# Loading the last sum of w2 into a separate buffer one unit sooner, and turning the last two quarter blocks together at the end: routing attention with a feed-forward block on one Trainium2 core

## The chip, the cores and the metric

The kernel runs on one core of a Trainium2 chip. A core has five engines, each with its own queue of instructions: TensorE (PE, with its weight loads shown as PEld), VectorE (DVE), ScalarE (ACT), GpSimd (POOL) and SyncE (SP). SP, ACT and POOL also issue transfers (DMA) between the device memory and the core's own memories: SBUF, from which the engines work, and PSUM, eight banks into which TensorE writes its sums. The metric is the time on the device in microseconds (us) of one execution.

## What is computed

```python
# attention: batch 4, 8 heads, 768 rows, 64 columns; a key counts where its nearest of 16
# centroids is the query's
mask = q_assign[:, :, :, None] == k_assign[:, :, None, :]
scores = np.where(mask, scale * q @ k.transpose(0, 1, 3, 2), -1e9)
attn = softmax(scores)
x = (attn @ v) as (4, 768, 512)
# feed-forward block, w_ch1 512x2048, w_ch2 2048x512
xn = (x - mean) / sqrt(var + 1e-6) * g_ln
out = x + np.maximum(xn @ w_ch1, 0.0) @ w_ch2
```

All of it is in 32-bit floats.

## The kernel before

**Stages.** First the attention of 16 pairs of heads (to 318 us of the span), then the feed-forward block for each batch b of 0 to 3, 768 rows each. Both products of the feed-forward block use fewer multiplications than the plain method: they are split into 2x2 blocks and done as seven block products (Winograd's form of Strassen's scheme), whose operands are sums and differences of blocks. For b of 1 to 3 the second product is split twice: seven products of seven products, 49 in all.

**The first product of a batch** runs in eight units j of 0 to 7 (`first_units`, L1355; `first_layer`, L897). In a unit TensorE makes seven products of 1.29 us each (L855, into the banks `x_ps`, `y_ps`, `z_ps`), ScalarE copies some of them out (L881) and applies the rectifier (L894, L922), and VectorE adds others (L886) and then makes sums of the hidden blocks (`outer_sums`, L1099 to L1102). Between the units stands `unit_end` (L1463), which for b = 1 does more: it prepares w2 for the second layers.

**Preparing w2 (b = 1).** Four sums of blocks of w2 were written to device memory earlier (`w2_keep`, into `w2_t`). Each comes back by `w2_back(i)` (L1040; one transfer of 1 MB issued by SP, L1042) into a buffer of the pool `splits` with tag "t", of which there is one. `w2_split(m, src)` (L1056) then makes four differences of it on VectorE (L1063, into the tile `wt`, two buffers) and stores them with one transfer of 1 MB issued by SP (L1064, into `w2_d`). The order over the units j = 0 to 6 is m = 1, 5, 3, 4, 2, 7, 6; m = 5, 4, 7, 6 read a sum that came back, m = 1, 3, 2 read w2 itself. Sum 1 is asked for ahead of the units, sums 4, 3 and 2 at the end of units 1, 3 and 5, after the split in that unit. In the profile's names digits are left out, so `w_t` stands both for the buffer and for the memory it is loaded from, `w_d` for `w2_d`.

**The second product** (`deep_layer`, L1227) goes through 49 steps (m, way); each is a `deep_product` (L1134) of 1.30 us on TensorE (L1146). Its weights come through a ring of ten slots filled by `ring_load` (L1080, one transfer of 256 KB, L1088, issued by SP). The first ten loads are asked for at the end of units 5, 6 and 7, the others one per step. After each step VectorE or ScalarE takes the bank out (L1159 copy, L1161 add), and `inner_sums` (L1120, L1122) and `inner_late` (L1127, L1129) make operands for later steps. Step (4, 1) stands ahead of the last work of the first layer, which follows as a job of steps (4, 1) and (4, 2).

**The buffers with tag "sums"** (pool `xpool`, two buffers of 128 x 2304 floats). In the first units of b = 1 one of them holds the sums `xt` of the input blocks. The other was last the tile `w2t`, read by TensorE (L963) in the second layer of b = 0. The next tile taken with this tag is `qs` in `inner_sums`, in unit 7.

**The end of the program** (b = 3). The outputs of the last m = 3 are sent out quarter by quarter by `last_part` (L1242). For ways 2 and 7 VectorE transposes a block of 32 x 32 pieces and four transfers send it (L1266, L1270). For ways 4 and 3, the last two steps, the quarter block lies in `end` (128 x 192, L1161); TensorE transposes its two halves through an identity (L1255) into the PSUM tile `turned`, VectorE copies the first half to `y_end` and ScalarE the second (L1259), and SP sends the first half and ACT the second (L1260, 48 KB each). `turned` comes from a PSUM pool of two banks (`ps_n`, L838), `y_end` from six buffers (`unit`).

**Order.** In this part of the program the instructions of PE, DVE, ACT and SP run in the order in which the code writes them; the waits between engines are put in by the framework, per tile. So a wait at the head of one queue holds up all that is written behind it on the same engine.

At the very end every engine loads the flag that tells whether a rarely used general path is needed (L1535) and branches over that path (L1536); then SP waits for the transfers and the other engines (L1759).

Of the kernel before, what the change touches and what calls it, by code (L numbers as in the profile page):

```python
# [23 lines left out]
def kernel(  # L24
# [49 lines left out]
    def ps(name, dt=F32, n=512):  # L74
        p = pools["long" if "long" in pools and name in ("x_ps", "z_ps") else "t"]
        return p.tile([P, n], dt, tag="t", name=name)
# [961 lines left out]
        nc.sync.dma_start(out=w2_t[i - 1], in_=t.rearrange("p h c f -> p (h c f)"))  # L1038

    def w2_back(i):  # L1040
        t = splits.tile([P, 2, NFH, P], F32, tag="t", name="w2_t")
        nc.sync.dma_start(out=t.rearrange("p h c f -> p (h c f)"), in_=w2_t[i - 1])  # L1042
        return t

    def w2_whole():

# [180 lines left out]
    def deep_layer(b, more, st):  # L1227

        done = {}

        def ahead_of(m):
            p = st[m] = {}
            onto = {2: 1, 3: 5}.get(m)
            p["add"] = done.get(onto)
            p["to"] = done[m] = done[onto] if onto else unit(f"m{m}")
            if m == ORDER[-1] and not more:
                p["ends"] = {}

        def sum_onto(i, j):
            nc.vector.tensor_tensor(done[i], done[i], done[j], ALU.add)  # L1240

        def last_part(o, way):  # L1242

            part = {2: (0, 0), 7: (1, 1), 4: (1, 0), 3: (0, 1)}.get(way)
            if part is None:
                return
            r, j = part
            queues = (nc.sync, nc.scalar, nc.gpsimd, nc.gpsimd) if way == 7 else (nc.sync, nc.scalar)
            if way in (4, 3):

                columns = st[ORDER[-1]]["ends"][way]
                turned, y = ps("turned"), unit("y_end")
                n = QC // 2
                for i in range(2):
                    nc.tensor.transpose(  # L1255
                        turned[:n, i * P : (i + 1) * P], columns[:, i * n : (i + 1) * n], ident
                    )
                    copy = (nc.vector.tensor_copy, nc.scalar.copy)[i]
                    copy(y[:n, i, :P], turned[:n, i * P : (i + 1) * P])  # L1259
                    (nc.sync, nc.scalar)[i].dma_start(  # L1260
                        out=out[b, r * QC + i * n : r * QC + (i + 1) * n, MH + j * P : MH + (j + 1) * P],
                        in_=y[:n, i, :P],
                    )
                return
            y = unit("y_end")[:, 0, :QC]
            nc.vector.transpose(y, o[:, j].rearrange("p (t a r) -> p t a r", a=2, r=Q)[:, :, r])  # L1266
            to = out[b].rearrange("(a r t) m -> a (r t) m", r=Q, t=NT)[r]
            for i in range(P // Q):
                m = MH + j * P + i * Q
                queues[i % len(queues)].dma_start(  # L1270
                    out=to[:, m : m + Q], in_=y[i * Q : (i + 1) * Q].rearrange("r (t f) -> r t f", f=Q)
                )

        def between():
            first_layer(b, NFH - 1, 3)
            relu(len(summed))
            outer_sums(NFH - 1, True)
            if more:
                norm_load(b + 1, 0)

        def s4(n):
            return lambda: outer_late((1, 1), (0, 1), "s", n)

        def norm(i, c):
            return lambda: norm_apply(b + 1, i, c)

        def rest(r, k, m):
            return lambda: add_rest(b, r, k, done[m])

        def out_of(r, k, m):  # L1290
            return lambda: turn(b, r, k, done[m])

        def onto(i, j):
            return lambda: sum_onto(i, j)

        jobs = {
            (4, 1): [lambda: first_layer(b, NFH - 1, 4)],
            (4, 2): [between],
            (4, 5): [lambda: rest_load(b, 0)],
            (4, 3): [rest(1, 0, 4)],  # L1300
            (7, 6): [s4(0)], (7, 4): [s4(1)], (7, 3): [s4(2)], (1, 6): [s4(3)],
            (1, 4): [onto(4, 7)], (6, 3): [onto(6, 1)],
            (5, 4): [onto(4, 6)], (5, 3): [onto(5, 6)], (2, 6): [onto(7, 5)],
        }
        for i, m in enumerate(ORDER[1:]):
            for n, way in enumerate((5, 7)):
                jobs.setdefault((ORDER[i], way), []).append(lambda m=m, n=n: inner_sums(st, m, (n,)))
        if more:
            for at, (i, c) in (
                ((4, 4), (0, 0)), ((7, 5), (0, 1)), ((1, 3), (0, 2)), ((6, 6), (0, 3)),  # L1310
                ((6, 5), (1, 0)), ((6, 4), (1, 1)), ((5, 6), (1, 2)), ((5, 5), (1, 3)),
            ):
                jobs.setdefault(at, []).append(norm(i, c))
            for at, c in (((4, 7), 1), ((7, 2), 2), ((7, 3), 3)):
                jobs.setdefault(at, []).append(lambda c=c: norm_load(b + 1, c))
            jobs[2, 4] = [out_of(1, 0, 4)]
            jobs[2, 3] = [rest(0, 0, 2), lambda: rest_load(b, 1)]
            jobs[3, 6] = [lambda: x_sum(b + 1, 1)]
            jobs[3, 5] = [lambda: w1_sums(b + 1, 0, (0, 1))]
            jobs[3, 7] = [lambda: first_layer(b + 1, 0, 1)]  # L1320
            jobs[3, 4] = [lambda: x_sum(b + 1, 2)]
            later(
                rest(1, 1, 7), out_of(1, 1, 7), out_of(0, 0, 2), None,
                rest(0, 1, 3), out_of(0, 1, 3), None,
            )
        else:
            jobs[7, 2] = [lambda: rest_load(b, 1)]
            jobs[1, 3] = [rest(1, 1, 7)]
            jobs[5, 6] = [rest(0, 0, 1), onto(4, 6)]
            del jobs[5, 4]  # L1330
            jobs[2, 5].append(rest(0, 1, 5))
            jobs[2, 1] = [out_of(1, 0, 4)]
            jobs[2, 7].append(out_of(1, 1, 7))
            jobs[2, 3] = [out_of(0, 0, 2)]

        for m, way in STEPS:
            if way == 1:
                ahead_of(m)
            deep_product(st, m, way)
            ring_load(b)  # L1340
            leave(2 if more else 4, (nc.sync,) if more else (nc.sync, nc.scalar))
            if way == 1:
                inner_late(st, m, way)
            for job in jobs.get((m, way), ()):
                job()
            if way == 2:
                inner_late(st, m, way)
            if m == 3 and not more:
                last_part(done[m], way)
        leave(len(leaving))  # L1350
        places[1, 1], places["e"] = places["e"], places[1, 1]

# [105 lines left out]
    with tc.manual_schedule(engines=order | {mybir.EngineType.SP}):  # L1458
# [4 lines left out]
        def unit_end(b, j):  # L1463

            if b + 1 < B:
                if j == 0:
                    rows_load(b + 1, 1)
                if j < NT:
                    norm_rows(b + 1, j)
            if b == 1:  # L1470
                leave(4)
                if j == 0:
                    outer["ends"] = all_in_range()
                if j == 2:
                    outer["flag"] = flag_of(outer.pop("ends"))
                m = (1, 5, 3, 4, 2, 7, 6, None)[j]
                if m in SUMS:
                    w2_split(m, outer.pop("t"))
                elif m:
                    w2_split(m, by_half(w2_block(*{1: (0, 0), 2: (1, 0), 3: (1, 1)}[m])))  # L1480
                if j in (1, 3, 5):
                    outer["t"] = w2_back({1: 4, 3: 3, 5: 2}[j])
                if j in (5, 6):
                    outer_late("s", "e", (0, 0), j - 5)
            while pending:
                job = pending.pop(0)
                if job is None:
                    break
                job()
            if b + 1 < B and j + 3 == NFH:  # L1490
                norm_stats(b + 1)
            if b + 1 < B and j + 2 == NFH:
                norm_stat_rows(b + 1)
            leave(4)
            if b == 1:
                if turning and j % 2 == 0:
                    columns_turn(row, lambda out, in_: leaving.append((out, in_)))
                elif asked and j % 2:
                    columns_load(row)
            if j > 4:  # L1500
                for _ in range(4):
                    if ring["next"] < len(STEPS) * (b - 1) + RING:
                        ring_load(b)

        for b in range(1, B):
# [1 line left out]
            if b + 1 < B:  # L1507
                rows_load(b + 1, 0)
            if b == 1:
                outer["t"] = w2_back(1)  # L1510
                first_units(b, 0)
            else:
                first_layer(b, 0, 2)
# [250 lines left out]
```

## Time and profile before

| what | us |
|---|---|
| median of 3 runs | 885.56 (885.01 to 886.95) |
| the profiled execution | 885.48 |
| its span, first to last instruction | 883.7 |
| PE busy in 534.20 to 552.00 (17.80 us) | 16.66 |
| DVE busy in 534.20 to 552.00 | 13.92 |
| PE busy in 552.00 to 600.00 (48.00 us) | 48.00 |
| PE busy in 600.00 to 740.00 (140.00 us) | 140.00 |
| PE busy in 740.00 to 872.00 (132.00 us) | 131.77 |
| PE busy in 872.00 to 884.00 (12.00 us) | 4.13 |

The span is the time from the first to the last instruction of one profiled execution; some 1.8 us of the execution's own time lie outside it. The table gives TensorE's busy time by stretches: where it is near the length of the stretch, TensorE had work all the time, and the difference is what it stood still. The granted clock was 1.00 in each of these stretches but the last.

### The profile page before, as it was taken

To read this page: it belongs to the slowest core of one execution; us is meant where nothing else is said; L and a number is where in the kernel's file an instruction comes from. 1 tells how busy PE (TensorE), PEld (TensorE's weight loads), DVE (VectorE), ACT (ScalarE), POOL (GpSimd) and SP (SyncE) were. 2 spreads that over 40 slices of the span, in tenths; PEclk is the share of its full clock that TensorE was granted. 3 is DMA by queue.
4 is the path that set the end of the run, shared out by engine and by line. 5 is a ranking of instruction groups with operands and counts; after the bars stand their busy time and mean duration, and the time that the engine had idled before them with its cause. 6 is when DMAs were issued, how large, how long until landed. Compare 5 with 4: busy or idle time off the path is not lost.

```text
span 883.7 us, 13207 instructions
## 1 busy us (share of the span) xinstructions
PE 871.6 (99%) x4648; PEld 574.7 (65%) x4648; DVE 704.5 (80%) x1149; ACT 402.8 (46%) x741; POOL 78.3 (9%) x143
## 2 busy tenths in 40 slices
PE   8999999999999999999999999999999999999996
PEld 5444444444444445568885557996557997557995
DVE  6899999999999878959577778997556897646774
ACT  6777788888898823330004542103552101333110
POOL 1012121222222212110000000000000000000000
PEclk9999999999999999999999999999999999999998
DMA  7777899999986338875685878854236862511874
GB/s 161 135 130 127 152 173 184 196 208 183 196 190 186 99 116 210 232 202 208 187 193 163 251 246 304 294 160 98 57 72 207 282 191 54 119 54 39 276 200 99
DMA packets 250426, 151.01 MB, mean 171 GB/s; under 512 B 192096, under 2 KB 207984, under 8 KB 249328
## 3 DMA queue, kind: packets, MB, share of 16 engines
q1 hardware_dynamic: 219216, 130.75, 56.1%
q0 software_dynamic: 7776, 15.03, 8.8%
q10 hardware_dynamic: 23360, 4.30, 2.7%
q8 instruction: 39, 0.64, 0.3%
q14 instruction: 35, 0.29, 0.1%
HBM read 108.40 MB, written 33.25 MB: 160 GB/s over the span
## 4 chain that ended last, share of the span: by engine, by line
PE 97%; DVE 1%; DMA 1%; ACT 0%; issue 0%; ACTq 0%
PE x_ps L855 18%; PE s_ps L401 18%; PE a_ps L413 14%; PE x_ps L1146 12%; PE z_ps L855 9%; PE z_ps L1146 6%; PE x_ps L963 5%; PE y_ps L855 5%; PE y_ps L1146 3%; PE z_ps L963 2%; PE sim_ps L320 1%; PE den_ps L469 1%; PE y_ps L963 1%; DMA k_sb<-in_k_dram 0%; DMA q_sb<-in_q_dram 0%; ACT lower L894 0%
## 5 line engine op out<-in xcount | busy, mean ns | idle before, releaser
L401 PE MATMUL s_ps<-t,t 64*128 64x384 f32 x768 | 154.8, 483 | 0.0
L401 PEld LDWEIGHTS s_ps<-t,t 64*128 64x128 f32 x768 | 68.0, 187 | 39.0 <-issue 38.3
L1146 PE MATMUL x_ps<-lower,w 128*128 128x192 f32 x448 | 80.9, 327 | 0.5 <-DVE u L1161 0.4
L1146 PEld LDWEIGHTS x_ps<-lower,w 128*128 128x128 f32 x448 | 74.1, 190 | 2.5 <-DVE u L1161 0.7
L886 DVE TENSOR_TENSOR lower<-z_ps,u 128x384 f32<-128x384 f32 x56 | 31.0, 553 | 53.1 <-PE z_ps L855 42.9
L396 ACT ACTIVATE e<-s_ps 128x768 f32<-128x768 f32 x84 | 67.0, 811 | 7.0 <-PE s_ps L401 6.4
L396 ACT ACTIVATE w<-s_ps 128x768 f32<-128x768 f32 x80 | 64.4, 811 | 8.3 <-PE s_ps L401 7.7
L894 ACT ACTIVATE lower<-lower 128x384 f32<-128x384 f32 x88 | 44.8, 521 | 45.9 <-DVE lower L886 45.8
L401 PE MATMUL s_ps<-mask,mask 64*128 64x384 bf16 x384 | 62.7, 323 | 1.0 <-ACT e L396 0.6
L881 ACT COPY u<-x_ps 128x384 f32<-128x384 f32 x64 | 30.5, 477 | 67.2 <-PE x_ps L855 67.1
L413 PE MATMUL a_ps<-e,v_sb 128*64 128x384 f32 x336 | 57.6, 488 | 0.0
L413 PE MATMUL a_ps<-w,v_sb 128*64 128x384 f32 x320 | 55.2, 488 | 0.0
L881 ACT COPY p<-x_ps 128x384 f32<-128x384 f32 x32 | 15.0, 470 | 83.6 <-PE x_ps L855 82.1
L855 PE MATMUL x_ps<-xn,ws 128*128 128x384 f32 x128 | 46.6, 487 | 0.0
L855 PE MATMUL x_ps<-xn,w 128*128 128x384 f32 x128 | 46.6, 487 | 0.0
L855 PE MATMUL x_ps<-xt,ws 128*128 128x384 f32 x128 | 46.6, 486 | 0.0
L855 PE MATMUL y_ps<-xn,w 128*128 128x384 f32 x128 | 46.5, 486 | 0.0
L855 PE MATMUL z_ps<-xt,ws 128*128 128x384 f32 x128 | 46.5, 486 | 0.0
L855 PE MATMUL x_ps<-xt,w 128*128 128x384 f32 x128 | 46.5, 486 | 0.0
L855 PE MATMUL z_ps<-xn,ws 128*128 128x384 f32 x128 | 46.5, 486 | 0.0
L1270 POOL DMA_DIRECT2D out_dram<-y_end x2 | 1.2, 597 | 487.5 <-DMA out_dram<-y 487.5
L413 PEld LDWEIGHTS a_ps<-e,v_sb 128*64 128x64 f32 x336 | 23.5, 137 | 31.8 <-issue 29.9
(232 smaller groups left out, 1679.4 us busy)
## 6 DMA issues: line engine op xcount, KB each, us to landing
w<-w_d SPq DMA_DIRECT2D x84, 256.0 KB, 3.2
raw<-in_moe_w_ch_dram SPq DMA_DIRECT2D x32, 512.0 KB, 4.7
w<-w_t SPq DMA_DIRECT2D x36, 256.0 KB, 5.1
w<-tb POOLq DMA_DIRECT2D x32, 256.0 KB, 5.4
w_d<-wt SPq DMA_DIRECT2D x7, 1024.0 KB, 5.6
w<-w_all SPq DMA_DIRECT2D x27, 256.0 KB, 2.8
v_sb<-in_v_dram SPq DMA_DIRECT2D x32, 192.0 KB, 5.2
xr<-x_d SPq DMA_DIRECT2D x24, 256.0 KB, 2.9
```

What stands on the lines that cost most here:

```text
L320: nc.tensor.matmul(sim[r : r + Q, :HC], cT[:, pr, :, :].rearrange("p j c -> p (j c)"), prepared[n][side][:, g * HC : (g + 1) * HC], start= ...
L396: nc.scalar.activation(e, s[:, :, :HC], AF.Exp, scale=SCALE)
L401: nc.tensor.matmul(s[:, j, :HC], of_keys[:, keys], of_queries[:, o : o + HC], start=part == first, stop=part != first, skip_group_check=True,)
L413: nc.tensor.matmul(acc[j * D : (j + 1) * D, :HC], loaded[n]["v"][:, j, c, :], e[:, j, :], start=(c == 0), stop=(c == NT - 1),)
L469: nc.tensor.matmul(den[r : r + Q, :HC], ones, sums[n, g][h][:, j, :], start=h == 0, stop=h == parts - 1, tile_position=(0, r), skip_group_ ...
L855: nc.tensor.matmul(bank[:, :HC], lhs[:, c, :], rhs[:, c], start=first and c == 0, stop=c == NDH - 1, skip_group_check=True,)
L881: nc.scalar.copy(t, bank[:, :HC])
L886: nc.vector.tensor_tensor(h, bank[:, :HC], other, ALU.add)
L894: nc.scalar.activation(h, h, AF.Relu)
L963: nc.tensor.matmul(bank[:, :MH].rearrange("p (h f) -> p h f", h=2), hidden[lhs + (c,)][:, tt * P : (tt + 1) * P], rhs[:, :, c], start=firs ...
L1146: nc.tensor.matmul(bank, w[:, c, :], a[:, c], start=way in (1, 2, 5) and c == 0, stop=c == NQH - 1, skip_group_check=True,)
L1270: queues[i % len(queues)].dma_start(out=to[:, m : m + Q], in_=y[i * Q : (i + 1) * Q].rearrange("r (t f) -> r t f", f=Q))
```

## The change

Three edits.

1. `w2_back` no longer returns its buffer but notes it under the sum's number, so that two may be under way. Sum 2, the last to come back, goes into a buffer with tag "sums" instead of the one with tag "t", and is asked for at the end of unit 4 instead of unit 5.
2. At the end, nothing is done after step (3, 4). After step (3, 3) `last_part` is called for way 4 and then for way 3.
3. In `last_part` each half gets its own PSUM tile `turned`, and the engines are dealt anew: both halves of way 4 are copied by ScalarE and sent by SP; of way 3 the first half is copied by VectorE and sent by SP, the second copied by ScalarE and sent by ACT, as before.

```diff
     def w2_back(i):
-        t = splits.tile([P, 2, NFH, P], F32, tag="t", name="w2_t")
+        if i == 2:
+            t = xpool.tile([P, 3, S], F32, tag="sums", name="w2_t", bufs=2).rearrange("p a s -> p (a s)")
+            t = t[:, : NFH * MH].rearrange("p (h c f) -> p h c f", h=2, c=NFH)
+        else:
+            t = splits.tile([P, 2, NFH, P], F32, tag="t", name="w2_t")
         nc.sync.dma_start(out=t.rearrange("p h c f -> p (h c f)"), in_=w2_t[i - 1])
-        return t
+        outer["t", i] = t
...
-                turned, y = ps("turned"), unit("y_end")
-                n = QC // 2
+                n, y = QC // 2, unit("y_end")
                 for i in range(2):
-                    nc.tensor.transpose(
-                        turned[:n, i * P : (i + 1) * P], columns[:, i * n : (i + 1) * n], ident
-                    )
-                    copy = (nc.vector.tensor_copy, nc.scalar.copy)[i]
-                    copy(y[:n, i, :P], turned[:n, i * P : (i + 1) * P])
-                    (nc.sync, nc.scalar)[i].dma_start(
+                    turned = ps("turned")
+                    nc.tensor.transpose(turned[:n, :P], columns[:, i * n : (i + 1) * n], ident)
+                    copy = nc.vector.tensor_copy if way == 3 and i == 0 else nc.scalar.copy
+                    copy(y[:n, i, :P], turned[:n, :P])
+                    (nc.sync if way == 4 or i == 0 else nc.scalar).dma_start(
...
             if m == 3 and not more:
-                last_part(done[m], way)
+                for part in {4: (), 3: (4, 3)}.get(way, (way,)):
+                    last_part(done[m], part)
...
                 if m in SUMS:
-                    w2_split(m, outer.pop("t"))
+                    w2_split(m, outer.pop(("t", SUMS.index(m) + 1)))
...
-                if j in (1, 3, 5):
-                    outer["t"] = w2_back({1: 4, 3: 3, 5: 2}[j])
+                if j in (1, 3, 4):
+                    w2_back({1: 4, 3: 3, 4: 2}[j])
...
             if b == 1:
-                outer["t"] = w2_back(1)
+                w2_back(1)
                 first_units(b, 0)
```

## Prediction

> **What bounds it now.** The page first: TensorE's busy time, and the chain that ended last.
>
> ```profile
> PE 871.6 (99%) x4648; PEld 574.7 (65%) x4648; DVE 704.5 (80%) x1149; ACT 402.8 (46%) x741; POOL 78.3 (9%) x143
> PE 97%; DVE 1%; DMA 1%; ACT 0%; issue 0%; ACTq 0%
> ```
>
> TensorE is the bound; only what it waits for, and what follows it at the end, can be won. Next, its waits, longest first (those over 0.6 us):
>
> ```profile
> PE turned L1255 <- DVE end L1161: 1.2, 2, 0.6
> PE y_ps L1146 <- ACT lower L894: 1.1, 1, 1.1
> PE idle_ps L700 <- DVE warm L176: 1.0, 1, 1.0
> PE turned L1255 <- DVE y_end L1259: 0.8, 2, 0.4
> ```
>
> The second must be traced back, through three timelines (start, duration, idle before and who ended it). TensorE's:
>
> ```profile
> 536.81 1.14 PE L1146 MATMUL y_ps<-lower,w 128*128 128x192 f32 x6
> 539.08 0.59 PE L1146 MATMUL y_ps<-lower,w 128*128 128x192 f32 x2 [1.13 <-ACT lower L894]
> 540.97 1.54 PE L1146 MATMUL x_ps<-lower,w 128*128 128x192 f32 x8
> 542.35 1.46 PE L1146 MATMUL z_ps<-qs,w 128*128 128x192 f32 x8
> ```
>
> VectorE's, which makes the hidden blocks for that step:
>
> ```profile
> 526.73 0.55 DVE L886 TENSOR_TENSOR lower<-z_ps,u 128x384 f32<-128x384 f32 x1
> 529.91 0.69 DVE L1063 TENSOR_TENSOR wt<-w_t 128x512 f32<-128x512 f32 x1 [2.62 <-DMA w_t<-w_t]
> ...
> 534.92 0.56 DVE L1099 TENSOR_TENSOR fifth<-lower 128x384 f32<-128x384 f32 x1 [0.59 <-ACT lower L894]
> ...
> 537.92 0.55 DVE L886 TENSOR_TENSOR lower<-z_ps,u 128x384 f32<-128x384 f32 x1
> ```
>
> And SP's, which asked for what VectorE waits for:
>
> ```profile
> 510.85 0.37 SPq L1064 DMA_DIRECT2D w_d<-wt  x1
> 515.01 2.13 SPq L1219 DMA_DIRECT2D x_d<-col  x4
> 521.91 0.38 SPq L1064 DMA_DIRECT2D w_d<-wt  x1
> 522.33 0.50 SPq L1042 DMA_DIRECT2D w_t<-w_t  x1
> ```
>
> Read from below: SP asks for sum 2 at 522.33, behind the 1 MB store of 521.91; it lands at 529.82 (landings are from the trace's records of completed transfers). VectorE, free since 527.29, stands 2.62 us. Everything behind its split comes late, to the add at 537.92; the rectifier of that block ends at 539.02, and TensorE, at the last chunk of step (4, 2), has waited. Last, the end on TensorE and ACT:
>
> ```profile
> 872.22 1.57 PE L1146 MATMUL x_ps<-lower,w 128*128 128x192 f32 x8 [0.45 <-DVE u L1161]
> 874.38 0.31 PE L1255 MATMUL turned<-ident,end 128*96 128x128 f32 x1 [0.59 <-DVE end L1161]
> 875.08 0.31 PE L1255 MATMUL turned<-ident,end 128*96 128x128 f32 x1 [0.38 <-DVE y_end L1259]
> 875.23 1.47 PE L1146 MATMUL z_ps<-lower,w 128*128 128x192 f32 x8
> 878.62 0.33 ACTq L1260 DMA_DIRECT2D out_dram<-y_end  x1
> ```
>
> Product (3, 3) stands behind two turns that wait for VectorE.
>
> **Part A, sum 2 earlier.** The same 1 MB load, none added. In SP's queue it is moved past the w_d store of 521.91 and the four x_d stores of 515.01, to directly behind the store of 510.85: issue at 511.3. ACT's and POOL's queues aren't passed. SP stands idle there until 515.01, so nothing in its queue waits longer, if the buffer is free. It is: its last tenant `w2t` was last read by TensorE (L963) at 454, and the other "sums" buffer, `xt`, read until 537, isn't touched. The next tenant, `qs` (written at 536.46), then waits for VectorE's own split only. Landing: 7.5 us after issue as now, 518.8; even the slowest landing of these transfers in the stretch, 8.8, gives 520.1, before 527.29. What the load displaces: the x_d stores land some 2.7 us later (sum 2 landed that much behind the store ahead of it, 527.13 to 529.82), and nobody reads them in this batch. The transfer that VectorE awaits at 514.01 (`col`, issued at 504.83, landed 513.88) is ahead of it in the queue and keeps its place.
>
> Now VectorE afresh from 527.29, with its own durations: split 2.54 us to 529.85, `outer_late` to 530.72, the y add to 531.18; then it waits for TensorE's z product (ends 531.80), adds to 532.37, waits for the rectifier to 532.95, `outer_sums` and `inner_sums` to 535.95, the last z add to 536.5. Rectified at 537.05, where TensorE asks at 537.79: the wait goes, with 0.7 us to spare (if that cover fails, each us of it costs one). Then `inner_sums` for the last chunk (537.09 to 537.82) and `inner_late` to 538.85; step (4, 6) would ask at 539.40. So that small wait goes too. What TensorE gains: from 536.81 to 542.35 it took 5.54; without waits it is 1.30 + 1.29 + 1.30 = 3.89 (products' starts lie 1.30 and 1.29 apart elsewhere). **1.65 us.** The low end is the wait as listed, 1.13; that nothing is won, or something lost, are rivals below. The nearest row to the value is the sum of the products itself, so I take the high end.
>
> What is late next? In the stage from 534 to 552 the transfers are busy 91%. I paired each ring load with its product: the load for (4, 7) lands at 542.84, 0.81 us before its use at 543.65; all others in this batch have 1.4 and more. TensorE comes there 1.65 earlier, at 542.0. But that load is issued at 537.95, behind a load that waits for the tiny statistics store queued behind the split's 1 MB store (532.56). That store moves 2.6 us earlier with VectorE, and with it these issues: landing near 540.2, 1.8 us to spare. From 552 on TensorE stands nowhere until 871.8, so the gain reaches the end.
>
> **Part B, the end.** Four turns, four copies and four stores remain; one copy goes from VectorE to ACT, one store from ACT to SP. Product (3, 3) follows (3, 4) directly: start 873.63 (872.22 + 1.41), last matmul done 875.09. `end` of way 4 was ready at 874.33, in its cover. The turns of way 4 run at 874.93 and 875.08 (0.15 is what follows a turn at 875.08); ACT's two copies (0.26 each) end at 875.56 and 875.82, and hold up nothing else on ACT, which stood idle 16 us; SP sends. `end` of way 3: 875.13 to 875.63 (0.50). Its first turn 875.68 to 876.0, VectorE's copy (0.29) to 876.32, SP's issue 876.38. Its second turn adds a wait, for the bank of way 4's second half, free at 875.82 (nothing stands behind it on TensorE): 875.87 to 876.18, ACT's copy to 876.48, ACT's issue 876.51 instead of 878.62. So ACT and TensorE end 2.11 earlier. SP's last issue was at 877.95, and is now third in a row (0.33 to 0.35 each, from 875.59), held by the copy: 876.38, **1.57 earlier**.
>
> After that 4.7 us pass in which no view shows work. The trace's records of branches and semaphores, which no view prints, show: each engine branches (VectorE 878.27, SP 878.33, TensorE 878.56, ACT 879.53), resumes 2.7 to 3.8 us later, and SP checks all transfers until 882.83. The last store's landing at 881.9 (3.3 after issue, most of it in 1.5) held SP 0.44 us. New: SP branches at 876.77, resumes at 879.46, needs 1.37 of unheld checks: 880.83, 2.0 earlier. The store lands by 879.8, in cover (879.95 is when SP would ask). POOL's drain, though, ended at 881.06 and depends on none of this: against 882.93 it allows 1.87. I take **1.9**, range 1.2 to 2.2. The far bounds: SP's issues at the 1.03 us that one took amid small-packet stores at 868.88 would put its last end 0.4 later than now; the nearest row, 0.34 for this very form, speaks for the other end.
>
> The Trainium skill, "DMA: Bandwidth & Descriptors", section "Issuing engines are not separate DMA queues", holds that all issuing queues share the same 16 DMA engines and several of them only save issue time: by it, a third store on SP costs one issue and nothing else, which the trace's 0.34 us puts inside the copy's wait. "Runtime: NRT & Kernel Launch", section "Instruction fetch mechanics", says that a taken branch to a page not held forces a fetch before going on; the 2.7 to 3.8 us after the branches agree, and by it the end would move with the latest branch, ACT's, by 2.1 rather than by 1.9.
>
> **Sum.** 1.65 + 1.9 = 3.55. The profiled execution took 885.48 (span 883.7 and 1.8 around it): 881.9; on the median of 885.56, **882.0**.
>
> **Rivals.**
> - *A is given back* (8%): the load or another late operand takes the wait's place. For: 0.81 us of slack now. Against: its issue moves more than its use. Time 885.56 - 1.9 = 883.7.
> - *The end doesn't move* (7%): fetches after the branches, or the landing among four stores within 1 us, set it. For: landings up to 4.4 us in this trace, a DMA share of 0.94 at 874 to 875. Against: 0.46 by 876. Time 885.56 - 1.65 = 883.9.
> - *The buffer isn't free and SP asks no sooner, nor does the end move* (3%): 885.6. The tenants' last reads speak against it.
> - *Slower* (4%): the ring runs dry at (4, 7). TensorE waits there for each us that the load lands after 542.0; to eat 3.55 and 1.8 more it must land after 547.3, against 542.84 now. Two bursts of 1 MB ahead of it (2.7 each, some 5.4) bring it to 548.2, 6.2 too late: 885.56 - 3.55 + 6.2 = 888.2. For: 91% busy transfers. Against: the 1 MB that stood just there is moved away.
>
> **The numbers.** 78% for the forecast, whose own range (A 1.13 to 1.65, B 1.2 to 2.2, 0.5 for the spread of medians) is 881.2 to 883.7. With the two lesser gains 8 in 10 lie in 880.9 to 884.0. About 0.2%, 1.8 us, can be told from no change, so faster means under 883.8: the forecast and more than half of the first rival, some of the second: 85%; same 11%; slower 4%.
>
> **What would show it.** VectorE's split of sum 2 starts near 527.3 with no wait for `w_t`; L1146's wait for L894 is gone; step (4, 6) starts near 539.4; product (3, 3) follows (3, 4) at 1.4; the last ACT issue comes 2.1 earlier relative to (3, 4). Wrong would be a wait of TensorE on a ring load near 542, or a gap of more than 4.9 us after the last issue.

## The result, and the profile after

| | before | changed |
|---|---|---|
| median of 11 runs each, us | 886.06 (885.01 to 887.16) | 883.25 (882.74 to 884.20) |
| the profiled execution, us | 885.48 | 882.89 |
| its span | 883.7 | 881.1 |
| start of the span to step (4, 1) | 534.22 | 534.56 |
| step (4, 1) to step (3, 4) | 338.00 | 336.29 |
| step (3, 4) to the end | 11.49 | 10.26 |

The ratio of the times is 0.9971, with a 95% interval of 0.9962 to 0.9980: 1.8 to 3.4 us less. Forecast was 882.0 in a range of 880.9 to 884.0, from a median before of 885.56 that came out 0.5 higher here. The last three rows are starts of TensorE's steps in the two traces. The first of them ends ahead of the first wait of TensorE that the change removes; in the kernels below it lies anywhere between some 534 and 535.6, with the new load or without, and this noise has to be taken out before two profiles are compared. What is left is a gain of 1.71 us in the middle (forecast 1.65) and of 1.23 us at the end (forecast 1.9).

**The page** (busy time with its share of the span and its instructions, then the chain that ended last):

```profile
PE 871.2 (99%) x4648; PEld 575.4 (65%) x4648; DVE 703.9 (80%) x1148; ACT 403.3 (46%) x742; POOL 77.9 (9%) x143
...
PE 99%; DVE 0%; ACT 0%; issue 0%; ACTq 0%
```

TensorE does the same work in 871.2 us, of a shorter span. One copy has gone from DVE to ACT (1149 to 1148 instructions, 741 to 742). TensorE's longest waits of 500 us and later are now these (line, whom it waits for; total, times, longest):

```profile
PE turned L1259 <- ACT y_end L1261: 0.5, 1, 0.5
PE x_ps L1150 <- DVE u L1165: 0.4, 1, 0.4
```

(Four lines were added ahead of them, so L1146, L1161 and L1255 are now L1150, L1165 and L1259.) The wait of 1.1 us for the rectifier L894 is gone, and so are the four waits of the turns for VectorE, 2.0 us in all. One wait of a turn for a bank has come, as the prediction said it would.

**The middle.** SP's timeline (start, duration), then VectorE's, then TensorE's:

```profile
511.18 0.37 SPq L1068 DMA_DIRECT2D w_d<-wt  x1
511.65 0.45 SPq L1046 DMA_DIRECT2D w_t<-w_t  x1
515.46 4.56 SPq L1223 DMA_DIRECT2D x_d<-col  x4
522.35 0.38 SPq L1068 DMA_DIRECT2D w_d<-wt  x1
...
530.75 1.90 SPq L608 DMA_DIRECT2D stat_d<-st  x1
535.54 0.80 SPq L611 DMA_DIRECT2D stat_row<-stat_d  x2
536.39 0.42 SPq L1092 DMA_DIRECT2D w<-w_d  x1
```

```profile
527.17 0.55 DVE L886 TENSOR_TENSOR lower<-z_ps,u 128x384 f32<-128x384 f32 x1
527.64 0.68 DVE L1067 TENSOR_TENSOR wt<-w_t 128x512 f32<-128x512 f32 x1
```

```profile
537.15 1.46 PE L1150 MATMUL y_ps<-lower,w 128*128 128x192 f32 x8
538.45 1.45 PE L855 MATMUL z_ps<-xn,ws 128*128 128x384 f32 x4
539.74 1.46 PE L1150 MATMUL x_ps<-lower,w 128*128 128x192 f32 x8
541.04 1.46 PE L1150 MATMUL z_ps<-qs,w 128*128 128x192 f32 x8
```

SP asks for sum 2 at 511.65, directly behind the store of unit 4. VectorE's split starts at 527.64, right after the add, with no bracket behind it: it waited for nothing. On TensorE the chunk y_ps, which was torn in two with 1.13 us between, is one group of eight, and the starts lie 1.29 to 1.30 apart.

**The end** (TensorE, VectorE, and the issues of SP and ACT):

```profile
870.85 1.57 PE L1150 MATMUL x_ps<-lower,w 128*128 128x192 f32 x8 [0.45 <-DVE u L1165]
...
872.26 1.46 PE L1150 MATMUL z_ps<-lower,w 128*128 128x192 f32 x8
...
873.56 0.38 PE L1259 MATMUL turned<-ident,end 128*96 128x128 f32 x2
873.76 0.50 DVE L1165 TENSOR_TENSOR end<-z_ps,u 128x192 f32<-128x192 f32 x1 [0.80 <-PE z_ps L1150]
...
874.15 1.49 SPq L1262 DMA_DIRECT2D out_dram<-y_end  x3
...
874.40 0.40 PE L1259 MATMUL turned<-ident,end 128*96 128x128 f32 x2 [0.46 <-ACT y_end L1261]
...
875.13 0.35 ACTq L1262 DMA_DIRECT2D out_dram<-y_end  x1
```

Product (3, 3) starts 1.41 us after (3, 4), and the last issue of ACT lies at 4.27 us after the start of (3, 4), where it was 6.40: 2.13 earlier, forecast 2.11. All of this went as predicted. But from the end of that issue, 875.48, to the end of the span, 881.1, there are 5.6 us, where there were 4.8: a good part of what was won ahead of the last issue is lost behind it.

### The profile page after: what moved, and what is told of

It is laid out like the page before. It is cut to its first block, busy times and chain, and to the rows that moved or that the text cites. A ratio compares the mean times of both kernels' runs of the same rounds, so it can differ in the third digit from the quotient of the medians.

```text
span 881.1 us, 13202 instructions
## 1 busy us (share of the span) xinstructions
PE 871.2 (99%) x4648; PEld 575.4 (65%) x4648; DVE 703.9 (80%) x1148; ACT 403.3 (46%) x742; POOL 77.9 (9%) x143
## 4 chain that ended last, share of the span: by engine, by line
PE 99%; DVE 0%; ACT 0%; issue 0%; ACTq 0%
PE x_ps L855 19%; PE s_ps L401 18%; PE a_ps L413 14%; PE x_ps L1150 12%; PE z_ps L855 9%; PE z_ps L1150 6%; PE x_ps L963 5%; PE y_ps L855 5%; PE y_ps L1150 3%; PE z_ps L963 2%; PE sim_ps L320 1%; PE den_ps L469 1%; PE y_ps L963 1%; PE idle_ps L700 0%; PE qk_ps L303 0%
## 5 line engine op out<-in xcount | busy, mean ns | idle before, releaser
L1150 PE MATMUL x_ps<-lower,w 128*128 128x192 f32 x448 | 80.8, 326 | 0.4 <-DVE u L1165 0.4
L1150 PEld LDWEIGHTS x_ps<-lower,w 128*128 128x128 f32 x448 | 74.2, 190 | 2.1 <-DVE u L1165 0.7
L894 ACT ACTIVATE lower<-lower 128x384 f32<-128x384 f32 x88 | 44.9, 521 | 43.7 <-DVE lower L886 43.7
```

Source lines behind the costliest of these rows:

```text
L894: nc.scalar.activation(h, h, AF.Relu)
L1150: nc.tensor.matmul(bank, w[:, c, :], a[:, c], start=way in (1, 2, 5) and c == 0, stop=c == NQH - 1, skip_group_check=True,)
```

## The experiments

The question is what becomes of the 2.1 us at the end, and which edit each gain belongs to. All times at the end are counted from the start of step (3, 4), so that kernels can be laid side by side; those of branches, landings and POOL's drain are from the trace's records of branches, semaphores and completed transfers, which no view prints. "Resumes" is SP's first instruction behind its branch, and POOL's drain is the long instruction in which POOL waits after its last work. In e10 and e11 that drain lay far ahead of the end: it was over at 496.3 and 393.4 us of the span.

| kernel | last issue | SP branches | SP resumes | last landing | POOL's drain ends | end |
|---|---|---|---|---|---|---|
| before | 6.40 | 6.11 | 8.80 | 9.72 | 8.83 | 11.49 |
| e1 load alone | 6.39 | 6.11 | 8.74 | 9.91 | 8.24 | 11.68 |
| e4 buffer only | 6.40 | 6.11 | 9.12 | 9.68 | 8.94 | 11.46 |
| changed | 4.27 | 4.84 | 8.02 | 8.29 | 8.60 | 10.26 |
| e12 changed, again | 4.27 | 5.17 | 8.30 | 7.95 | 8.74 | 10.54 |
| e2 end alone | 4.27 | 4.98 | 8.10 | 8.27 | 9.05 | 10.33 |
| e3 stores as before | 4.27 | 4.57 | 7.15 | 8.66 | 8.23 | 10.43 |
| e5 deferral alone | 5.02 | 4.73 | 7.46 | 8.65 | 9.04 | 10.43 |
| e13 deferral, again | 5.02 | 4.73 | 7.42 | 8.62 | 8.90 | 10.39 |
| e6 banks alone | 5.28 | 5.57 | 8.22 | 9.59 | 9.08 | 11.43 |
| e10 no POOL stores | 4.27 | 5.08 | 8.13 | 8.12 | none here | 10.37 |
| e8 no general path | 4.27 | none | none | 6.30 | 8.70 | 9.49 |
| e9 branch elsewhere | 4.27 | none here | none here | 5.99 | 8.89 | 9.72 |
| e11 e8 and e10 | 4.49 | none | none | 6.39 | none here | 7.73 |

One rule, whose constants are fitted to these eleven ends, holds for every kernel with the branch at the end (to 0.02 us, e6 to 0.06): the end is 0.88 us after the later of two things, SP's resuming plus 1.36, and the last landing plus 0.9. In the changed kernel these are 9.38 and 9.19; in the one before, 10.16 and 10.62.

### e1: the earlier load alone

```diff
 # the changed kernel, with last_part and its call as before
-                for part in {4: (), 3: (4, 3)}.get(way, (way,)):
-                    last_part(done[m], part)
+                last_part(done[m], way)
```

> The load of sum 2 from unit 4 into its own buffer, the end as before. Theory (the two parts add up; the load is worth its full 1.65 us, the end was over-priced): 1.7 us under the kernel before, some 884.4 where that takes 886.1; from step (4, 1) to step (3, 4) 336.3 us instead of 338.0, and 11.5 us from there to the end as before. Rival (the load's gain is partly given back later and the end's is whole): under 1.2 us gained, and more than 336.7 between these steps.

Median 884.21 against 886.00 in the same runs: ratio 0.9983 [0.9974, 0.9992], 1.8 us. From (4, 1) to (3, 4) it took 336.55, 1.45 less than before; the end stayed (11.68). TensorE's longest waits are again those of the turns, and none is for L894:

```profile
PE turned L1259 <- DVE end L1165: 1.2, 2, 0.6
PE idle_ps L700 <- DVE warm L176: 1.0, 1, 1.0
PE turned L1259 <- DVE y_end L1263: 0.8, 2, 0.4
```

The middle gain belongs to edit 1 alone. The 0.26 us that are missing against the changed kernel's 336.29 were lost at (4, 7), in TensorE's timeline:

```profile
540.62 1.46 PE L1150 MATMUL z_ps<-qs,w 128*128 128x192 f32 x8
542.10 2.84 PE L1150 MATMUL x_ps<-lower,w 128*128 128x192 f32 x16
```

The two starts lie 1.48 apart instead of 1.30. The load of (4, 7) landed at 541.97, and TensorE, due there at 541.92, went on only behind it. That is the rival of a dry ring, for a quarter of a microsecond; the gap is too short to stand in the list of waits.

### e2: the new end alone

```diff
 # the kernel before, with last_part and its call as in the changed kernel
-                last_part(done[m], way)
+                for part in {4: (), 3: (4, 3)}.get(way, (way,)):
+                    last_part(done[m], part)
```

> The new end alone, the load as before. Theory: the end is worth 1.2 to 1.3 us: 884.8 where the kernel before takes 886.1; from step (3, 4) to the end 10.2 to 10.3 us instead of 11.5, and still 338.0 from (4, 1) to (3, 4), with the wait of 1.1 us in step (4, 2). Rival (the end is worth the 1.9 us forecast, and the profiled execution of the changed kernel had a slow end by chance): 9.6 us from (3, 4) to the end.

Median 884.75 against 886.00: 0.9987 [0.9978, 0.9996], 1.25 us, and 10.33 from (3, 4) to the end. The middle has gained nothing, with 338.51 and the old wait:

```profile
PE y_ps L1146 <- ACT lower L894: 1.2, 1, 1.2
```

So the end is worth some 1.2 us by itself, in its own trace (11.49 to 10.33) as in its times, and not 1.9. The two parts add up: 1.79 and 1.25 are 3.04, against 2.81 for both together.

### e4: the other buffer, asked for no sooner

```diff
 # e1, with the order of the requests as before
-                if j in (1, 3, 4):
-                    w2_back({1: 4, 3: 3, 4: 2}[j])
+                if j in (1, 3, 5):
+                    w2_back({1: 4, 3: 3, 5: 2}[j])
```

> Sum 2 gets its own buffer but is asked for at the end of unit 5 as before; the end as before. Theory (what counts is the place of the load in SP's queue behind the 1 MB store of unit 5, not the buffer): no gain, within 0.3 us of the kernel before; VectorE's wait of 2.6 us for the load and TensorE's of 1.1 us in step (4, 2) are still there. Rival (the old buffer, shared with sum 3, held the load up): the waits shrink and 0.8 us or more is gained.

Median 885.87 against 886.00: 0.9999 [0.9990, 1.0008], no difference that can be measured. VectorE's timeline shows the old wait for the load, and TensorE's list of waits what it leads to:

```profile
526.55 0.55 DVE L886 TENSOR_TENSOR lower<-z_ps,u 128x384 f32<-128x384 f32 x1
529.63 0.69 DVE L1067 TENSOR_TENSOR wt<-w_t 128x512 f32<-128x512 f32 x1 [2.52 <-DMA w_t<-w_t]
```

```profile
PE y_ps L1150 <- ACT lower L894: 0.7, 1, 0.7
```

The wait is 0.4 shorter than before in this execution, which the times don't bear out as a gain. The second buffer brings nothing by itself. It is what lets two sums be under way; the earlier request is what brings the time.

### e3: stores dealt as before

```diff
-                    (nc.sync if way == 4 or i == 0 else nc.scalar).dma_start(
+                    (nc.sync, nc.scalar)[i].dma_start(
```

> The changed kernel, but each half of way 4 sent as before the change, the first by SP and the second by ACT. Theory (SP's third issue, 0.58 us instead of 0.34, makes its branch late): SP's last issue back at 0.34, its branch some 0.25 us sooner after (3, 4), the end 0.1 to 0.25 us sooner, 10.0 to 10.15 us after (3, 4), as the landing of the last store is next. Rival (the longer time from SP's branch to its next instruction, 3.19 us instead of 2.69, sets it, whoever issues): no difference over 0.05 us in when SP resumes; 10.25 us.

Median 883.06 against 886.00: 0.9966 [0.9952, 0.9979], no different from the changed kernel. SP's two issues took 0.33 each, it branched 0.27 sooner, as expected, and resumed 0.87 sooner, yet the end came at 10.43, not at 10.0 to 10.15: the expectation failed, and so did its rival (no change in when SP resumes), because now the last landing, at 8.66, sets it (8.66 + 0.9 + 0.88 = 10.44). A gain at SP is taken away by the landing. That the order of the two can change from kernel to kernel is why the two rows must both be kept.

### e5 and e13: deferral alone

```diff
 # the changed kernel, with last_part as before and the new call kept
-                    turned = ps("turned")
...
-                    copy = nc.vector.tensor_copy if way == 3 and i == 0 else nc.scalar.copy
...
+                turned, y = ps("turned"), unit("y_end")
...
+                    copy = (nc.vector.tensor_copy, nc.scalar.copy)[i]
...
+                    (nc.sync, nc.scalar)[i].dma_start(
```

> The changed kernel, but in each quarter block both halves share one PSUM tile and are copied and sent as before the change; the turns still stand behind step (3, 3). Theory (deferring takes 1.6 us out of TensorE's way, the shared tile then costs a wait of each second turn for VectorE's copy): step (3, 3) starts 1.4 us after (3, 4); the last copy and issue come 0.9 to 1.0 us later than in the changed kernel, some 5.2 us after (3, 4), and the end 0.8 to 1.0 us later, 11.1 us after (3, 4); 884.1 in time. Rival (deferring alone is all of the gain): the end at 10.3 after (3, 4).

Median 882.93 against 886.22: 0.9963 [0.9952, 0.9973]. TensorE at the end of e5, and ACT's last issue:

```profile
872.08 1.46 PE L1150 MATMUL z_ps<-lower,w 128*128 128x192 f32 x8
873.38 0.27 PE L1259 MATMUL turned<-ident,end 128*96 128x128 f32 x1
874.25 0.42 PE L1259 MATMUL turned<-ident,end 128*96 128x128 f32 x2 [0.60 <-DVE y_end L1263]
875.05 0.31 PE L1259 MATMUL turned<-ident,end 128*96 128x128 f32 x1 [0.38 <-DVE y_end L1263]
...
875.70 0.33 ACTq L1264 DMA_DIRECT2D out_dram<-y_end  x1
```

With one bank for both halves the turns wait for the copies again, and the last issue comes at 5.02, 0.75 later than in the changed kernel (expected 0.9 to 1.0). The end does not: 10.43, not 11.1. The theory that the end follows the last issue falls here. SP had branched at 4.73, ahead of that issue, and the last store still landed at 8.65, as in e3.

To see whether the own banks bring anything at all, the changed kernel and this one were run again side by side. The first needed no edit, the second is e5 under another name:

> The changed kernel itself, to be set beside the next one on the same chip. Both theories: 883.2 with the kernel before at 886.1.

> The changed kernel with both halves of a quarter block in one PSUM tile and copied and sent as before the change (deferral alone) once more. Theory now (the end hangs on fetches and late landings, not on the last issue, so that the 0.75 us by which own banks bring that issue forward are not seen): within 0.3 us of the changed kernel in the same call. Rival (own banks do count, and the earlier run was lucky): 0.7 us or more slower than the changed kernel.

Medians 882.97 and 882.86, both 0.9965 [0.9951, 0.9978] of the same runs of before. In this kernel edit 3, the own banks and the new dealing, has no effect that can be measured beside the deferral.

### e6: own banks and the new dealing, no deferral

```diff
-                for part in {4: (), 3: (4, 3)}.get(way, (way,)):
-                    last_part(done[m], part)
+                last_part(done[m], way)
```

> The changed kernel, but the quarter block of way 4 is turned straight after step (3, 4), ahead of (3, 3) as before; each half has its own PSUM tile and the engines are as in the changed kernel. Theory: the turns wait for VectorE's add only (0.6 us after the product), the second follows at once, so step (3, 3) starts 2.4 us after (3, 4) (3.0 before, 1.4 in the changed kernel); the last issue is 5.2 to 5.3 us after (3, 4) and the end 0.9 to 1.0 us later than in the changed kernel; 884.2 in time. Rival (own banks alone are all of the gain): the end at 10.3 after (3, 4).

```profile
870.34 1.57 PE L1150 MATMUL x_ps<-lower,w 128*128 128x192 f32 x8 [0.45 <-DVE u L1165]
872.50 0.42 PE L1259 MATMUL turned<-ident,end 128*96 128x128 f32 x2 [0.59 <-DVE end L1165]
872.76 1.47 PE L1150 MATMUL z_ps<-lower,w 128*128 128x192 f32 x8
```

One wait, of 0.59 for `end`, stands ahead of product (3, 3) instead of two, so (3, 3) starts 2.4 after (3, 4), and the last issue comes at 5.28: both as expected. The end was expected at 11.2 and came at 11.43, no better than before, held by a landing at 9.59. The times say otherwise: 883.54 against 886.22, 0.9966 [0.9956, 0.9977], a gain of 2.7 of which the load explains 1.8. The one profile and the medians differ by 0.6 to 0.9 here. Most of that lies with the kernel before: its profiled execution took 885.48, 0.74 under its median in these runs, while e6's, 883.54, lies at its own. Where a usual execution of the kernel before spends these 0.7 us, and so whether the new dealing gains at the end without the deferral, the profiles don't show.

### e8: the branch over the general path taken out

```diff
-    usual = nc.values_load(flag[0:1, 0:1], min_val=0, max_val=1)
-    with tc.If(usual == 0):
-        whole_weights(tc, [weight_chunk(m) for m in range(NWC)])
-        with tc.For_i(0, B, 1) as b:
-            general(tc, b, q, k, v, out, cT, rev, eps, ident, g_sb, w1, w2)
```

> The changed kernel without the general path, its branch and the loading of the flag: it leaves out the fallback for inputs out of range, which these inputs do not take. Theory (after the last issue the end waits for code that the branch makes each engine fetch, and the last landings are late because they run into these fetches): SP goes on to its checks within 0.2 us of its last issue; the last store lands whole by 6.5 us after (3, 4) instead of 8.1 to 8.3; the end is then set by POOL's drain, which has taken 6.2 us from 2.4 after (3, 4): 9.4 us after (3, 4) instead of 10.3, 882.4 in time. Rival 1 (the late landings have nothing to do with the branch): the last landing stays at 8.1 or more. Rival 2 (POOL's drain itself waits for such a fetch): it ends sooner too, and the end is at 8.3 or less.

The last issue is at 4.27, as in the changed kernel, but the last landing is at 6.30 instead of 8.29. The last two stores land 1.9 and 2.1 us after their issue, while in all kernels with the branch at the end the last one to land took 3.3 to 4.4. The end, at 9.49, is 0.8 after POOL's drain, as the theory had it. Median 882.23 against 886.22: 0.9956 [0.9944, 0.9969]. In its profile the end is 0.77 sooner than in the changed kernel, but the middle took 336.87, 0.58 longer; the list of TensorE's waits puts 0.3 us of that down to a standstill before an x_ps product for which no releaser is seen:

```profile
PE x_ps L1150 <- issue: 0.3, 1, 0.3
```

Its cause stays open.

### e9: a short path behind the branch

```diff
     with tc.If(usual == 0):
-        whole_weights(tc, [weight_chunk(m) for m in range(NWC)])
-        with tc.For_i(0, B, 1) as b:
-            general(tc, b, q, k, v, out, cT, rev, eps, ident, g_sb, w1, w2)
+        nc.vector.memset(g_sb, 0.0)
```

> The changed kernel with one small fill of a constant in place of the general path, so that the flag is loaded and the branch is there but passes over little code: it leaves out the fallback for inputs out of range, which these inputs do not take. Theory (it is the distance of the branch, that is, code not yet held, that costs, not the branch): each engine resumes within 0.5 us of its branch instead of 2.9 to 4.3; the end 9.4 to 9.8 us after (3, 4). Rival (the branch or the loading of the flag costs by itself): resumption still 2 us or more after the branch, and the end within 0.3 us of the changed kernel's 10.3.

Median 881.94 against 886.22: 0.9947 [0.9930, 0.9964]. In the trace the branch isn't at the end: the framework moved it with its short path to between 713 and 717 us (POOL's to 491), and TensorE's branch there took 0.24 us. So it doesn't tell a near branch from a far one at the same place, as it was meant to. What it does show is the end of e8 once more: no branch in the last stretch, landing at 5.99, POOL's drain at 8.89, end at 9.72.

### e10 and e11: POOL's last stores taken away, with the branch and without

```diff
-            queues = (nc.sync, nc.scalar, nc.gpsimd, nc.gpsimd) if way == 7 else (nc.sync, nc.scalar)
+            queues = (nc.sync, nc.scalar)
```

> The changed kernel, but the four stores of the quarter of way 7 go out on SP and ACT, none on POOL. Theory (the end is set by the fetches after the branches, SP's resumption 8.0 us after (3, 4) and the late last landings at 8.1 to 8.7): POOL's branch leaves the end, the others' stay; the end 10.0 to 10.3 us after (3, 4), within 0.3 us of the changed kernel. Rival (POOL's part in the end, its fetch or its drain, is what delays the others): the end at 9.6 or less.

> The same without the general path, its branch and the loading of the flag: it leaves out the fallback for inputs out of range, which these inputs do not take. Theory (without the branch, POOL's drain set the end at 9.5; it runs on for some 7 us after POOL's last transfers): without these transfers it is over long before; SP's checks end 6.2 to 6.5 us after (3, 4), the end is at 7.1 to 7.4, the time 880.0 to 880.6. Rival (something else holds the end at 9.5): no gain over the kernel without the general path alone.

With the branch, e10: 883.82 against 886.21, 0.9976 [0.9965, 0.9986], and the end at 10.37 (expected 10.0 to 10.3): no gain over the changed kernel, which took 882.97 in the same runs. With no store to send at the end, POOL drained long before, and the end didn't move. Without the branch, e11: 880.22, 0.9935 [0.9922, 0.9949], the end at 7.73 (expected 7.1 to 7.4) and the time within the 880.0 to 880.6 expected. It comes 1.34 after the last landing at 6.39. POOL's drain is thus the next bound, but only once the branch is gone.

No kernel that computes all that is asked for is measurably faster than the changed one.

## Why the prediction was right, and where it was off

**Right:** the direction, the time (883.25, forecast 882.0) and part A to its working. 1.71 us were gained between (4, 1) and (3, 4), for 1.65 worked out from the products' distances, and e4 shows that the way to it is the one described: no earlier request, no gain. Of the signs named, the split without a wait, the missing wait for L894, (4, 6) at 539.74 (forecast near 539.4, plus the 0.34 that this execution was late), (3, 3) 1.41 after (3, 4), and the last issue of ACT 2.13 earlier have all come.

**One cover in part A was over-estimated.** The forecast gave the load for (4, 7) 1.8 us to spare; it landed at 541.46, 0.88 ahead of its use, about as before (0.81). In the other kernels with edit 1 it landed anywhere from 1.9 us ahead of the use to late (e1). The step was that SP's statistics store moves 2.6 us earlier "and with it these issues". The w_d store ahead of it moved 2.28, from 532.56 to 530.28, but the statistics store, 0.46 long before, took 1.90 in the changed kernel (SP's lines above), so `stat_row` went out 1.52 earlier and the load 1.56. In this execution no time was lost by it.

**Mis-sized: part B, 1.9 forecast, 1.23 measured.** The step that failed reads: "SP branches at 876.77, resumes at 879.46, needs 1.37 of unheld checks: 880.83, 2.0 earlier. The store lands by 879.8, in cover". Relative to (3, 4), its parts came out as follows.

- *SP's third issue in a row.* It came 1.52 earlier (forecast 1.57), but took 0.58 instead of 0.33, and SP branched 1.27 earlier, not 1.57. In the others where it is third in a row it took 0.38 to 0.91 (e2 0.73, e12 0.91, e9 0.38); where it is second, in e3 and e5, and in e6, where it stands apart from the two ahead of it, 0.32 to 0.33.
- *Resuming took longer.* 3.19 us from SP's branch to its next instruction, where it was 2.69. So SP resumed only 0.78 earlier. It took 3.06 to 3.19 in the four profiles with the branch in which SP sends three halves in a row (changed, e2, e10, e12), and 2.58 to 2.73 in e3, e5 and e13. But e6, where the three aren't in a row, took 2.65, and e4, with the old end, 3.00. What sets it is not shown.
- *The landing was in cover*, as forecast: 8.29, ahead of SP's check of it. With it went the 0.44 us by which the landing held SP before. That was luck in part: the landing was forecast at 7.6 after (3, 4) and came 0.7 later, and it stayed in cover because SP resumed as late (8.02, forecast 7.24). With SP as forecast, by the rule above, the landing would have set the end, at 10.07.
- The sum is -1.27 + 0.50 - 0.44 = -1.21, against the 1.23 measured. The forecast gain was 3.55 in all and the medians show 2.81; 0.67 of the 0.74 between them is this part.

**Two statements more did not hold.** The forecast cut 2.0 to 1.9 because POOL's drain "ended at 881.06 and depends on none of this". In the changed kernel it ended at 8.60, with the end at 10.26; e10 took it away from the end and the end stayed, at 10.37. It doesn't bind here. And the 4.9 us after the last issue that I named as a sign of a wrong end did occur, at 5.6: it counts from ACT's issue, which e5 shows not to be what the end follows.

**What the end does follow.** In the kernels with the branch it is SP's resuming or the last landing, whichever is later, and by the rule above the two lie only 0.1 to 1.1 us apart, now the one ahead and now the other. Taking the branch out, with the path behind it and the loading of the flag, brought the last landing from 3.3 or more to 1.7 to 2.1 us after its issue (e8, e9, e11).

For the landing the trace's records of packets tell more. Such a store is 112 packets. In each of the eleven kernels with the branch at the end, 105 packets of a last store go first, and the other 7, a sixteenth, start within 0.05 us of the end of one packet of 16 KB in an instruction queue. In the changed kernel that packet is in flight from 875.96 to 877.70; of ACT's last store, 105 packets have started by 876.35 and the 7 start from 877.65 on, and 7 of SP's follow behind them. In e8, e9 and e11 there is no such packet, and the 112 go together. So the late landing is a sixteenth of the store that stands behind a fetch of instructions, as far as times can show it; the records do not say which DMA engine carried which packet. The 16 KB packet starts 0.93 to 0.95 us after TensorE's branch in nine of the eleven (1.18 in e3, 1.27 in e12).

For SP's resuming, the fetch of the instructions behind the branch is the likeliest reading (packets of 8 to 16 KB in the two instruction queues are in flight from 875.0 to 877.7 in the changed kernel), but it is inferred: the one kernel that was to vary the distance (e9) moved the branch. And not every engine pays: POOL, which branches over the same path at 2.15 to 2.35 where it sends stores at the end, goes on 0.2 us later.

The Trainium skill, "Runtime: NRT & Kernel Launch", section "Instruction fetch mechanics", says that a taken branch to code not held forces a fetch. The 2.6 to 4.5 us of PE, DVE, ACT and SP between branch and next instruction agree, and they are gone in e8; POOL's 0.2 us show that not every such branch costs them. My use of it, that the end would move with the latest branch, by 2.1, was wrong: 1.23 was measured.

**The rivals.** That the end doesn't move at all (883.9) fell by e2, 1.25 us less, with an interval that excludes no change. That part A is given back fell by e1. The dry ring didn't come in the changed kernel's profile, where 0.88 us of cover was left; it came in e1's, for a quarter of a microsecond.

## What to carry to other kernels

When a late operand stalls a chain, look for the request in its queue first: a second buffer was worth nothing here (e4), the earlier request 1.8 us (e1). At a program's end, work out each of the last conditions separately (the queue that checks the transfers, the last landing, each engine's drain) and take their latest; 2.1 us won ahead of the last issue gave 1.2 here. Test an edit made of several by its parts: the own banks and the new dealing cost code and brought nothing that could be measured beside the deferral.

## What the runs showed of the hardware that was not expected

- With a branch over a long unused path right after them, the last store of 48 KB to land took 3.3 to 4.4 us from its issue; without it 1.7 to 2.1 (e8, e9, e11). What is late is 7 of a store's 112 packets; the first such 7 start when a packet of 16 KB in an instruction queue ends (eleven kernels of eleven).
- Four engines that branch there resumed after 2.6 to 4.5 us: PE 3.7 to 4.5, DVE 3.1 to 3.4, ACT 2.6 to 3.1, SP 2.6 to 3.2. POOL, which branches some 2 us earlier, resumed after 0.2.
- POOL's drain ended 8.2 to 9.1 us after (3, 4), 6.6 to 7.5 us after the start of POOL's last issue at 1.62, in every kernel in which POOL sent something at the end. Without such stores it was over some 370 us and more ahead of the end (e10, e11). With the branch the drain hides; without it, POOL's two stores cost 1.8 us (e8 9.49, e11 7.73).
- An issue of one of these halves on SP took 0.32 to 0.38 us alone, first or second, and 0.38 to 0.91 as the third in a row (e2, e8 to e12 and the changed kernel).
